# An order computed inside the kernel, and transposes moved to DMA, in a fused attention and feed-forward kernel

## The chip, the cores and the metric

The kernel runs on one core of one Trainium2 chip. The metric is the device time of one execution in microseconds (us); less is better. Each kernel was executed several times. A verdict of faster or slower needs a difference of 2%, with a 95% interval.

Names used below: PE is the matrix engine TensorE, PEld its weight loads, DVE is VectorE, ACT is ScalarE, POOL is GpSimd and SP is SyncE. SP computes nothing here; it issues DMA transfers. A letter q after an engine's name means its instruction queue.

## The reference, cut to what matters

The input `x` is 2048 x 512, in bf16. The output mixes an attention layer with memory (32 heads of width 16, four segments of 512 tokens) and a gated feed-forward layer (width 1792), with one gate value per token.

```python
g = sigmoid((x * gate_w).sum(-1))
for s in range(4):                                   # segments of 512 tokens
    p = softmax(q_s k_s^T * scale + causal mask);  a_dot = p v_s
    a_mem = phi(q_s) M / (phi(q_s) z + 1e-6)         # phi(t) = t+1 if t>0 else exp(t)
    o_s = sigmoid(beta) * a_mem + (1 - sigmoid(beta)) * a_dot
    M += phi(k_s)^T v_s;  z += sum phi(k_s)
a = o @ wo
b = (relu(x @ W_gate) * (x @ W_up)) @ W_down
out = g * a + (1 - g) * b
```

## The kernel before

A "unit" is one segment and one group of eight heads, so there are 16 units. Each unit computes scores K·Q on PE into one four-bank tile of PSUM (the accumulators' memory), takes exp of them on ACT, masks on POOL, multiplies by V on PE, combines on DVE and transposes back on PE. That is the score chain. Since it has only one four-bank tile, a fill (the score matmuls) and its exp alternate and never overlap. Other work (projections, gate and up matmuls, down matmuls) has to fill the engines in between. The framework's pools decide which buffers are shared:

```python
# PSUM: "S" one 4-bank tile for scores; "X" 2 banks; "F" 2 banks
def xT_and_gate(seg):                         # x^T by PE transposes
    for c in range(NC):
        tp = psum.tile([P, 4, P], BF16, name="tp", tag="F", bufs=2)
        for t in range(4):
            nc.tensor.transpose(tp[:, t, :], xn[:, t, c * P:(c + 1) * P], ident[:])
        nc.vector.tensor_copy(xT[:, c, seg * L:(seg + 1) * L], ...)

def proj(seg):
    ...                                       # Q; then K, dimension-major:
    for c in range(NC):
        ps = psum.tile([P, L], F32, name="ps_proj", tag="X", bufs=2)
        ...                                   # 4 matmuls wk, xT
        nc.vector.tensor_copy(KTe[:, c, :], ps[:])
        ...
    if seg < NSEG - 1:                        # K a second time, token-major, for phi(K)
        for t in range(4):
            ps = psum.tile([P, D], F32, name="ps_proj", tag="X", bufs=2)
            for ci in range(NC):
                nc.tensor.matmul(ps[:], lhsT=xT[:, ci, s0 + t * P:s0 + (t + 1) * P],
                                 rhs=wk_sb[:, ci, :], ...)
            ...                               # exp, min, max-add -> pK
    ...                                       # V

def qk_exp(seg, c):                           # 6 fills of the score tile per unit
    for kb in range(4):
        Nk = L - P * kb                       # 512, 384, 256, 128 columns
        if Nk > 256:
            for r in range(2):
                sp = psum.tile([P, 4, L], F32, name="sp", tag="S", bufs=1)
                ...                           # 4 matmuls of 32 rows, exp, mask
        else:
            ...                               # both r in one fill

for i, u in enumerate(units):                 # emission order of the main loop
    seg, c = u
    if i + 1 < len(units):
        pending_E[un] = qk_exp(*un)           # scores of the next unit
    if c == 1 and seg < NSEG - 1:             # the whole next projection, in one block
        xT_and_gate(seg + 1); proj(seg + 1); tok_gate(seg + 1)
        gate_gen[seg + 1] = ffn_gateup_items(seg + 1)
    pv_combine(seg, c, pending_E.pop(u), hook=hook)   # hook: gate/up and down matmuls
    ...
```

The softmax here doesn't subtract the row's maximum and nothing guards it: scores larger than these inputs give would overflow.

## Time and profile before

| | before |
|---|---|
| median of 3 runs | 353.75 us (353.05 to 354.65) |
| span of the profiled execution | 351.7 us |
| PE busy | 308.4 us (88%) |
| first exp of the score chain starts | 30.0 us |
| last exp ends | 329.3 us, so the chain takes 299.3 us for 96 fills |
| after the last exp | 22.4 us |

The profile page first. The first lines give busy time and share of the span by engine. The rows of digits cut the span into 40 slices; a digit is the busy share in tenths, and PEclk is PE's granted clock. The last line is the chain of waits, followed back from the end.

```profile
span 351.7 us, 7235 instructions
...
PE 308.4 (88%) x2941; PEld 148.1 (42%) x2992; DVE 229.1 (65%) x684; ACT 198.0 (56%) x187; POOL 90.5 (26%) x153
...
PE   3489988899999799898999988888999989989984
...
DVE  2557959788422756989835575899845386766253
...
PE 52%; DVE 30%; ACT 7%; DMA 5%; issue 3%; POOL 0%; SPq 0%; DVEq 0%; ACTq 0%
```

PE is busy, but often only at 8 tenths, and 30% of the chain of waits is DVE. PE's largest waits, by what ended them (total us, times, longest):

```profile
PE ndt L343 <- DVE o_sb L342: 9.8, 17, 1.4
PE tp L174 <- DMA xn<-in_A_x_dram: 5.7, 1, 5.7
PE ups L383 <- DMA wu_sb<-in_B_W_up_dram: 5.0, 1, 5.0
```

PE loses about 11 us at the start to two transfers, and 9.8 us in 17 small waits where the transpose of an output block waits for DVE. Now two stretches of the span. The columns are busy us and instructions of PE, PEld, DVE, ACT and POOL, then clock, DMA share and GB/s.

```profile
8.00:20.00 12.00, 6.02 (x26) 2.29 (x25) 5.47 (x15) 3.12 (x6) 0.00 (x0) 0.97 1.05 348
145.00:168.70 23.70, 21.60 (x184) 10.56 (x186) 21.69 (x62) 8.39 (x14) 3.97 (x6) 1.00 0.07 24
```

From 145 to 168.7 us (the projection of a new segment) DVE is busy for 21.69 of 23.7 us, ACT for only 8.39. What the score chain does is shown by ACT's timeline (start, length, instruction, and in brackets the idle time before it and what ended it):

```profile
148.10 1.02 ACT L286 ACTIVATE E_1851<-sp 128x1024 bf16<-128x1024 f32 x1 [0.50 <-PE sp L255]
...
165.00 0.60 ACT L387 ACTIVATE rg<-gps 128x512 bf16<-128x512 f32 x1 [2.07 <-PE ndt L343]
168.69 1.88 ACT L276 ACTIVATE E_2271<-sp 128x2048 bf16<-128x2048 f32 x1 [3.10 <-PE ndt L317]
...
171.07 1.88 ACT L276 ACTIVATE E_2271<-sp 128x2048 bf16<-128x2048 f32 x1
```

Between the exp at 148.10 and the one at 168.69 there is none for 19.6 us; ACT runs only small pieces of other work. Two full exps of a unit can start 2.4 us apart (168.69 to 171.07); over the whole chain a step takes 3.1 us on average (299.3 us for 96).

### The profile page before, as it was taken

Reading aid. Unit: us, or ns where it says so; the run is one execution under the profiler, and the core shown is the slowest. Engines: PE = TensorE matmul, PEld = TensorE weight load, DVE = VectorE, ACT = ScalarE, POOL = GpSimd, SP = SyncE. Lnnn points to the kernel's source line nnn. Section 1 sums busy time; section 2 is a strip of 40 time slices with the busy share of each in tenths; the row PEclk is TensorE's granted clock in tenths of the full one; section 3 lists DMA queues with packets and bytes.
Section 4 is the critical chain, followed back from the end, with each engine's and each line's share of the span. In section 5 each row is a group of like instructions: output and inputs, shape, how many; then the busy total and the mean of one; then the engine's idle time right before and its main releaser. Section 6 shows DMA issues by size and latency. Waiting matters only on the chain.

```text
span 351.7 us, 7235 instructions
## 1 busy us (share of the span) xinstructions
PE 308.4 (88%) x2941; PEld 148.1 (42%) x2992; DVE 229.1 (65%) x684; ACT 198.0 (56%) x187; POOL 90.5 (26%) x153
## 2 busy tenths in 40 slices
PE   3489988899999799898999988888999989989984
PEld 2133343335444344334644444334544444444452
DVE  2557959788422756989835575899845386766253
ACT  1306578755843687831754577841764378886300
POOL 6000343341321424310231144230231133242300
PEclk9989999999999999999999999999999999999999
DMA  7991100001000000001000000000000000000000
GB/s 195 357 335 55 61 2 0 2 1 62 3 16 16 32 2 0 2 0 61 2 2 17 30 18 3 0 2 0 2 3 17 30 17 2 0 2 3 0 32 30
DMA packets 10209, 12.39 MB, mean 35 GB/s; under 512 B 593, under 2 KB 9313, under 8 KB 10177
## 3 DMA queue, kind: packets, MB, share of 16 engines
q1 hardware_dynamic: 7584, 6.82, 6.1%
q0 software_dynamic: 1008, 3.55, 3.3%
q10 hardware_dynamic: 1584, 1.57, 1.4%
q8 instruction: 23, 0.38, 0.4%
q14 instruction: 10, 0.07, 0.1%
HBM read 9.84 MB, written 2.10 MB: 34 GB/s over the span
## 4 chain that ended last, share of the span: by engine, by line
PE 52%; DVE 30%; ACT 7%; DMA 5%; issue 3%; POOL 0%; SPq 0%; DVEq 0%; ACTq 0%
PE acc L398 14%; PE ups L383 9%; PE gps L378 7%; PE ndt L317 6%; DMA wu_sb<-in_B_W_up_dram 5%; PE sp L255 4%; DVE hT L388 4%; DVE tb L339 3%; DVE osb L411 3%; PE ps_proj L242 2%; PE ndt L343 2%; PE acc L408 2%; DVE coef L337 2%; PE ps_proj L230 2%; DVE rsb L335 2%
## 5 line engine op out<-in xcount | busy, mean ns | idle before, releaser
L383 PE MATMUL ups<-xT,wu_sb 128*128 128x512 bf16 x210 | 62.7, 382 | 7.1 <-DMA wu_sb<-in_B_W_up_dram 5.0
L378 PE MATMUL gps<-xT,wg_sb 128*128 128x512 bf16 x205 | 59.8, 380 | 2.3 <-DMA wg_sb<-in_B_W_gate_dram 1.0
L388 DVE TENSOR_TENSOR hT<-ups,rg 128x512 bf16<-128x512 f32 x56 | 38.3, 684 | 24.2 <-PE ups L383 18.5
L387 ACT ACTIVATE rg<-gps 128x512 bf16<-128x512 f32 x56 | 33.5, 598 | 35.7 <-PE gps L378 27.8
L398 PE MATMUL acc<-wd_sb,hT 128*128 128x512 bf16 x217 | 50.3, 379 | 0.9 <-DVE osb L411 0.2
L398 PEld LDWEIGHTS <-hT 128*128 128x128 bf16 x224 | 21.5, 98 | 25.3 <-issue 1.2
L383 PEld LDWEIGHTS <-wu_sb 128*128 128x128 bf16 x224 | 20.1, 98 | 25.5 <-DMA wu_sb<-in_B_W_up_dram 5.5
L345 DVE CAST oT<-ndt 128x128 bf16<-128x128 f32 x64 | 18.3, 286 | 16.4 <-PE ndt L343 16.4
L411 DVE TENSOR_SCALAR osb<-acc,ngcol 128x512 bf16<-128x512 f32 x16 | 12.0, 750 | 22.5 <-PE acc L408 22.5
L378 PEld LDWEIGHTS <-wg_sb 128*128 128x128 bf16 x224 | 18.3, 97 | 18.2 <-issue 3.7
L343 PE MATMUL ndt<-diag_134,o_sb 128*128 128x128 bf16 x64 | 14.5, 226 | 11.4 <-DVE o_sb L342 9.8
L333 DVE TENSOR_TENSOR dsb<-ndt,epsvec 128x16 f32<-128x16 f32 x48 | 8.1, 169 | 24.2 <-PE ndt L317 23.7
L255 PE MATMUL sp<-QTsb,KTe 32*128 32x512 bf16 (+3 forms) x256 | 21.7, 304 | 0.7 <-issue 0.2
L339 DVE TENSOR_TENSOR tb<-ndt,coef 128x256 bf16<-128x256 f32 x48 | 20.2, 421 | 1.3
L255 PE MATMUL sp<-QTsb,KTo 32*128 32x512 bf16 (+3 forms) x256 | 20.2, 299 | 0.6 <-ACT E_3100 L276 0.2
L408 PE MATMUL acc<-wo_sb,oT 128*128 128x512 bf16 x60 | 17.8, 380 | 2.3 <-DVE oT L345 1.9
L218 PE MATMUL ps_proj<-xT,wk_sb 128*128 128x512 bf16 x64 | 17.1, 396 | 2.3 <-DVE KTe L221 0.9
L242 PE MATMUL ps_proj<-wv_sb,xT 128*128 128x512 bf16 x62 | 15.7, 379 | 2.6 <-DVE pK L236 1.1
L343 PEld LDWEIGHTS <-o_sb 128*128 128x128 bf16 x64 | 6.1, 95 | 27.6 <-DVE o_sb L342 23.1
L204 PE MATMUL ps_proj<-xT,wq_sb 128*128 128x512 bf16 x61 | 17.1, 393 | 0.5
L255 PEld LDWEIGHTS <-KTe 32*128 32x128 bf16 x256 | 7.1, 91 | 24.1 <-issue 22.9
L207 DVE CAST QTsb<-ps_proj 128x512 bf16<-128x512 f32 x16 | 10.8, 685 | 3.8 <-PE ps_proj L204 3.8
(468 smaller groups left out, 708.6 us busy)
## 6 DMA issues: line engine op xcount, KB each, us to landing
out_dram<-osb SPq DMA_DIRECT2D x16, 128.0 KB, 1.7
xn<-in_A_x_dram POOLq DMA_DIRECT2D x3, 512.0 KB, 3.8
wd_sb<-in_B_W_down_dram POOLq DMA_DIRECT2D x2, 640.0 KB, 12.4
wg_sb<-in_B_W_gate_dram SPq DMA_DIRECT2D x2, 512.0 KB, 14.2
wu_sb<-in_B_W_up_dram SPq DMA_DIRECT2D x2, 512.0 KB, 18.2
wg_sb<-in_B_W_gate_dram SPq DMA_DIRECT2D x2, 384.0 KB, 13.2
wu_sb<-in_B_W_up_dram SPq DMA_DIRECT2D x2, 384.0 KB, 8.8
xn<-in_A_x_dram SPq DMA_DIRECT2D x1, 512.0 KB, 4.9
```

Of the source, the lines that this page charges most:

```text
L242: nc.tensor.matmul(ps[:], lhsT=xT[:, ci, s0 + t * P:s0 + (t + 1) * P], rhs=wv_sb[:, ci, :], start=(ci == 0), stop=(ci == NC - 1))
L255: nc.tensor.matmul(out_ap, lhsT=ktile[32 * j:32 * j + 32, c, kb * P:(kb + 1) * P], rhs=st["QTsb"][32 * j:32 * j + 32, c, kb * P:kb * P + N ...
L317: nc.tensor.matmul(ndm[:, 0, hl8, 0:DH + 1], lhsT=E[kb][:, es, (qb - kb) * P:(qb - kb + 1) * P], rhs=st["Vp"][:, kb, h, 0:DH + 1], start=f ...
L339: nc.vector.tensor_tensor(tb[:], ndm[:, :, :, 0:DH], coef[:, :, :, None].to_broadcast([P, 2, 8, DH]), ALU.mult)
L343: nc.tensor.matmul(trp, lhsT=o_sb.rearrange("p h e -> p (h e)"), rhs=diag16[:, t, :], start=True, stop=True)
L378: nc.tensor.matmul(gps[:], lhsT=wg_sb[:, ci, fv * P:(fv + 1) * P], rhs=xT[:, ci, s0:s0 + L], start=(ci == 0), stop=(ci == NC - 1))
L383: nc.tensor.matmul(ups[:], lhsT=wu_sb[:, ci, fv * P:(fv + 1) * P], rhs=xT[:, ci, s0:s0 + L], start=(ci == 0), stop=(ci == NC - 1))
L387: nc.scalar.activation(rg[:], gps[:], ACT.Relu)
L388: nc.vector.tensor_tensor(hT[:, fv, :], ups[:], rg[:], ALU.mult)
L398: nc.tensor.matmul(acc[:], lhsT=hT[:, fv, lc:lc + P], rhs=wd_sb[:, fv, :], start=(fv == 0), stop=False)
L408: nc.tensor.matmul(acc[:], lhsT=oT[:, ci, lc:lc + P], rhs=wo_sb[:, ci, :], start=False, stop=(ci == NC - 1))
L411: nc.vector.tensor_scalar(osb[:], acc[:], ngcol[:, tt:tt + 1], None, ALU.mult)
```

## The change

The intent is to keep PE busy without gaps. The kernel no longer leaves the order to the framework. It describes all work as tasks with an engine, a duration, a key of priority and dependences; a list scheduler in the kernel then fixes the order of every engine and the choice of PSUM banks. The score chain of a unit gets keys two units early (`LEAD`), so it always goes first; gate, up, down and projections are the filler. Along with this:

- x^T comes by a transposing DMA, and so does token-major phi(K), which makes the second K projection (48 matmuls) needless.
- Five full fills (4 x 512 columns) per unit take the place of six partly short ones: 80 in all, not 96.
- Four PSUM banks are one pool for all work outside the score tile; rings for Q, K, E and h are deeper.
- The token gate moves from DVE to 64 one-column matmuls; combines take two query blocks at once; one copy of 512 columns takes the place of four for o^T.
- The first weights are split, several weights move to the GpSimd queue, and nine warm-up matmuls run first.

The diff, cut to its core (cuts are marked `...`):

```diff
-HP = 18
+RQ = 6
+RE = 8
+RH = 18
+class Plan:
+    def run(self):
+        ...
+                for t in sorted((t for t in ready if t.avail <= now), key=lambda t: t.key):
+                    if busy.get(t.eng, 0.0) > now:
+                        continue
+                    if t.need is not None and not t.need.banks:
+                        got = self.pick(t.need, now)
+                        ...
+                    order.append(t)
+    ...
+    ctx.enter_context(tc.manual_schedule())
...
+    clock = [3000.0]
+    def arrival(nbytes):
+        clock[0] += nbytes / 380.0
+        return plan.add("in%d" % len(plan.tasks), 0.0, 0.0, None, lat=clock[0])
+    def load_xT(seg):
+        nc.sync.dma_start_transpose(out=xT[:, :, seg * L:(seg + 1) * L],
+                                    in_=x[seg * L:(seg + 1) * L, :])
+        return arrival(L * D * 2)
...
-    load_x(nc.sync, 0)
-    load_w_piece(nc.scalar, wq_sb, A_wq, 0, D)
-    load_w_piece(nc.scalar, wk_sb, A_wk, 0, D)
-    load_w_piece(nc.scalar, wv_sb, A_wv, 0, D)
...
+    got_x[0] = load_xT(0)
+    got_q = [load_cols(nc.scalar, wq_sb, A_wq, 0, 256)]
+    got_k = [load_cols(nc.scalar, wk_sb, A_wk, 0, 256)]
...
+    got_v = load_cols(nc.sync, wv_sb, A_wv, 0, D)
+    got_g[0] = load_cols(nc.sync, wg_sb, B_W_gate, *FP[0])
+    got_u[0] = load_cols(nc.sync, wu_sb, B_W_up, *FP[0])
+    got_x[1] = load_xT(1)
+    for i in range(1, 4):
+        got_g[i] = load_cols(nc.gpsimd, wg_sb, B_W_gate, *FP[i])
+        got_u[i] = load_cols(nc.gpsimd, wu_sb, B_W_up, *FP[i])
+    got_x[2] = load_xT(2)
+    got_x[3] = load_xT(3)
+    got_d = [load(nc.gpsimd, wd_sb[:, a:b, :], ...) for a, b in ((0, 7), (7, NF))]
+    got_o = load_cols(nc.gpsimd, wo_sb, A_wo, 0, D)
...
-            pK = segpool.tile([P, 4, D], BF16, name="pK", bufs=2)
-            for t in range(4):
-                ...
-                    nc.tensor.matmul(ps[:], lhsT=xT[:, ci, s0 + t * P:s0 + (t + 1) * P],
-                                     rhs=wk_sb[:, ci, :], ...)
+        prj["pk", seg, c] = plan.add("SP", 1300, key + 500, lambda: nc.sync.dma_start_transpose(
+            out=pK[i][:, :, c * P:(c + 1) * P], in_=pk[0][:]),
+            [b] + [att.get(("mz", seg - 2))], 2000)
...
+    FILLS = [[(0, 0, 0)], [(1, 0, 0)], [(0, 1, 0), (0, 3, 384)], [(1, 1, 0), (1, 3, 384)],
+             [(0, 2, 0), (1, 2, 256)]]
...
+    LEAD, FLAG, RL = 2.0, 0.0, 40000.0
+    for k in range(9):
+        nc.tensor.matmul(wb[3][:], lhsT=junk[:, 0:P], rhs=junk[:], start=True, stop=True)
+    order = plan.run()
+    for t in order:
+        if t.emit is not None:
+            t.emit()
```

The plan assumes that transfers land one after another in the order in which they are written down, at 380 bytes per ns from 3 us on.

## The prediction

> **What bounds the kernel now.** The page gives a span of 351.7 us with TensorE (PE) 88% busy, DVE 65%, ACT 56%; the chain of waits is 52% PE and 30% DVE. I count work, not busy time. In the timeline dense 128x512 matmuls start 216 ns apart, 32 P·V matmuls take 0.81 us, and a score fill of four 32-row tiles holds PE about 0.33 us, or 0.43 us where it cuts into other work. The Trainium skill ("TensorE: Matmul & The Clock Gate", "Wait — 56ns, not 53.3ns?") states 215.7 ns for 512 columns; this trace agrees. My PE sum for before is about 290 us. The missing 60 us: about 12 us in the first 20 us (windows view: PE busy 8.2 us, waiting for x, then the up weights), 6 us in the last 27 us, and about 40 us in between (11.4 us before the transposes of o, for DVE).
>
> **What the change removes and adds, estimated.**
> - PE: minus 48 second-K-projection matmuls (10.4 us) and 64 x transposes (0.71 us per 8: 5.7 us), plus 64 one-column gate matmuls (1.6 us). New sum: gate/up 97, down 48, four projections 55, scores 80 x 0.43 = 34, P·V 33, rest 11: about 278 us.
> - DVE: minus x^T copies (6.5), gate reductions (12.5), part of the combines (62.7 to about 48), of the oT copies (18.3 to 11), of the memory update (12 to 4): 229 to about 190 us.
> - ACT: five full fills of 1.88 us per unit (150 us in all) replace 9.55 us per unit; total 198 to about 195. The score chain is serial through one 4-bank tile: 80 x (1.88 + 0.43 + 0.35 signalling) = 213 us, about 260 with residual waits for a busy PE and ACT. It nears the PE bound, not more.
> - DMA transposes: 4 of 512 KB, 12 of 128 KB. The skill ("DMA: Bandwidth & Descriptors", "Latency and other measured facts") gives 261 GB/s, so an estimate of 2 us plus overhead for x; no trace shows one yet. The x load of before landed in 4.9 us; I expect 5 to 9.
>
> **What is on the critical path.** PE is nearly saturated, so the 14.5 us removed from it count fully; DVE work counts only through bubbles. The pinned order puts gate/up, down and the next projections as filler behind the score chain, with interchangeable banks and deeper rings. I expect 25 to 30 us of the 40 us of middle bubbles to go. Smaller first weight pieces and no PE transpose save 3 to 4 us at the start.
>
> **Prediction.** 278 PE + 10 start + 3 tail + 7 bubbles = **298 us, range 287 to 314**. Chances: faster by over 2% 0.96, within 2% 0.02, slower 0.02.
>
> **What would show it right.** PE busy well over 90% from about 12 us to the end; DVE about 190 us, ACT about 195; PE's largest wait in the middle no longer the o transposes; the chain mostly PE; x^T landing under 9 us; phi(K) transposes done long before the memory update.
>
> **What would make it wrong.** A pinned order cannot react: if a transfer lands later than planned, PE stands at the head of its queue though other work is ready. The x transpose could take 15 us. The score chain could be the bound, with ACT at every fill behind relu: then about 310. With nearly no bubbles: about 288.

## The result, and the profile after

| | before | after |
|---|---|---|
| median of the runs made side by side | 353.63 us (353.05 to 354.65) | 312.74 us (312.32 to 312.97) |
| ratio | | 0.8838 (0.882 to 0.8856): faster |
| span profiled | 351.7 us | 311.0 us |
| PE busy | 308.4 (88%) | 290.3 (93%) |
| DVE busy | 229.1 | 185.1 |
| ACT busy | 198.0 | 192.7 |
| first exp starts | 30.0 | 22.1 |
| first exp to last exp | 299.3 (96 fills) | 258.1 (80 fills) |
| after the last exp | 22.4 | 30.8 |

All outputs are right. Here and below, "gain" is the difference of medians, 353.63 - 312.74 = 40.9 us. The last three rows sum up to the span, so they split the 40.7 us by which the span fell: 7.9 from an earlier start of the score chain, 41.2 from a shorter chain, and 8.4 given back after it.

The page of after, the same lines (with the clock and the GB/s rows, which matter now):

```profile
PE 290.3 (93%) x2953; PEld 140.9 (45%) x2953; DVE 185.1 (60%) x458; ACT 192.7 (62%) x166; POOL 96.2 (31%) x150
...
PE   5646799999999999999999999999999999999995
...
DVE  0236287957688153977884549594879271838211
...
PEclk9989599999999999999999999999999999999999
...
GB/s 135 257 333 342 193 25 37 34 2 4 19 0 36 2 34 37 2 17 2 13 6 19 36 18 19 3 0 2 2 0 2 20 19 34 2 0 2 2 34 34
...
PE 80%; DMA 8%; DVE 7%; SPq 2%; ACT 1%; issue 1%; DVEq 0%; ACTq 0%
```

From the sixth slice on PE stands at 9, to the last slice but one. The weak part is the first five slices, 39 us, and these are also the slices with the most DMA traffic. The chain of waits is now 80% PE, and its second item is DMA. PE's waits:

```profile
PE wb_124 L321 <- DMA xT<-in_A_x_dram: 5.0, 1, 5.0
PE wb_125 L391 <- DMA wv_sb<-in_A_wv_dram: 4.6, 1, 4.6
PE wb_125 L321 <- DMA xT<-in_A_x_dram: 4.2, 1, 4.2
...
PE sp L404 <- ACT E_160 L425: 0.3, 1, 0.3
```

The three waits that matter are all for transfers at the start: x^T of segment 1 (5.0 us), the V weights (4.6) and x^T of segment 0 (4.2). Nothing after them is over 0.3 us (a wait of 1.9 us for a memset at the very start aside). The 9.8 us of waits for the o transposes are gone. By stretches:

```profile
0.00:10.00 10.00, 4.02 (x9) 1.34 (x10) 0.72 (x7) 1.28 (x1) 6.10 (x12) 1.00 0.95 128
10.00:20.00 10.00, 5.44 (x16) 1.87 (x15) 3.52 (x7) 1.31 (x3) 6.29 (x10) 1.00 1.09 327
20.00:33.30 13.30, 8.21 (x48) 3.02 (x49) 6.26 (x17) 4.35 (x3) 1.85 (x2) 0.78 1.07 323
33.30:36.00 2.70, 2.69 (x13) 0.67 (x13) 0.16 (x1) 0.79 (x2) 0.00 (x0) 0.50 1.70 182
...
50.00:300.00 250.00, 248.48 (x2688) 124.06 (x2686) 161.46 (x395) 173.76 (x147) 77.64 (x119) 1.00 0.06 13
```

PE is busy for 248.48 of 250 us from 50 to 300, but from 0 to 33.3 only for 17.7 us, and some of that is warm-up. In 33.3 to 36.0, after the wait of 5.0 us, the granted clock is 0.50. The Trainium skill ("TensorE: Matmul & The Clock Gate", "What's actually happening") says that the array falls to half its clock after an idle window of about 3.4 us; this trace agrees. ACT's timeline in the middle, where before had its gap:

```profile
143.98 1.88 ACT L425 ACTIVATE E_158<-sp 128x2048 bf16<-128x2048 f32 x1 [1.66 <-PE sp L404]
...
147.31 1.87 ACT L425 ACTIVATE E_159<-sp 128x2048 bf16<-128x2048 f32 x1
...
150.66 1.87 ACT L425 ACTIVATE E_160<-sp 128x2048 bf16<-128x2048 f32 x1
...
153.68 1.87 ACT L425 ACTIVATE E_161<-sp 128x2048 bf16<-128x2048 f32 x1
```

An exp starts about every 3.2 us while a new segment's projections run alongside. That is also the mean step of the whole chain (258.1 us for 80), no shorter than before's 3.1: the chain is shorter because it has fewer steps and no long gaps, while its exps are all full ones. In the whole chain after has one gap of over 3 us between exps (7.8 us at 28.0 us, while PE waits for x^T), before had 11.

Why were the transfers late? The timeline of the start: some of the issues (start, length of the issue, queue that issues), and the first matmuls that need x^T:

```profile
0.81 1.40 SPq L186 DMA_TRANSPOSE xT<-in_A_x_dram  x1
...
2.28 2.06 SPq L177 DMA_DIRECT2D wv_sb<-in_A_wv_dram  x1
...
2.78 0.75 POOL L177 DMA_DIRECT2D wg_sb<-in_B_W_gate_dram  x1
...
7.68 29.40 SPq L186 DMA_TRANSPOSE xT<-in_A_x_dram  x3
10.04 1.86 PE L321 MATMUL wb_125<-xT,wq_sb 128*128 128x512 bf16 x4 [4.16 <-DMA xT<-in_A_x_dram]
```

And the share of the queues (packets, MB), with q1 the queue of SP and q0 that of GpSimd:

```profile
q1 hardware_dynamic: 18736, 7.34, 11.6%
q0 software_dynamic: 1424, 4.99, 5.0%
```

Landing times, read from the trace per tile: x^T of segment 0 at 10.0 us (9.2 us after its issue), the V weights at 20.1 (issued at 2.28), the first gate and up pieces at 27.2 and 31.2, x^T of segment 1 at 33.3 (25.6 us after its issue at 7.68). In the same time six gate and up pieces on the GpSimd queue, none of them needed yet, landed at 14 to 22 us. So late-needed data went ahead of urgent data.

### The profile page after: what moved, and what is told of

It is laid out like the page before. It is cut to its first block, busy times and chain, and to the rows that moved or that the text cites. A ratio compares the mean times of both kernels' runs of the same rounds, so it can differ in the third digit from the quotient of the medians.

```text
span 311.0 us, 6988 instructions
## 1 busy us (share of the span) xinstructions
PE 290.3 (93%) x2953; PEld 140.9 (45%) x2953; DVE 185.1 (60%) x458; ACT 192.7 (62%) x166; POOL 96.2 (31%) x150
## 3 DMA queue, kind: packets, MB, share of 16 engines
q1 hardware_dynamic: 18736, 7.34, 11.6%
q0 software_dynamic: 1424, 4.99, 5.0%
## 4 chain that ended last, share of the span: by engine, by line
PE 80%; DMA 8%; DVE 7%; SPq 2%; ACT 1%; issue 1%; DVEq 0%; ACTq 0%
PE wb_123 L550 9%; DMA xT<-in_A_x_dram 8%; PE wb_122 L573 8%; PE sp L404 8%; PE wb_125 L550 7%; PE wb_124 L550 6%; PE wb_122 L550 6%; PE wb_123 L573 6%; PE wb_124 L453 4%; PE wb_122 L453 3%; PE wb_122 L586 2%; PE wb_123 L321 2%; PE wb_122 L321 2%; PE wb_124 L321 2%; PE wb_123 L586 2%; SPq L177 2%
## 5 line engine op out<-in xcount | busy, mean ns | idle before, releaser
L550 PEld LDWEIGHTS <-wg_sb 128*128 128x128 bf16 x224 | 20.0, 97 | 23.4 <-issue 3.2
L550 PEld LDWEIGHTS <-wu_sb 128*128 128x128 bf16 x224 | 18.8, 98 | 23.1 <-issue 7.0
L425 ACT ACTIVATE E_154<-sp 128x2048 bf16<-128x2048 f32 x10 | 18.7, 1874 | 9.6 <-PE sp L404 8.3
L425 ACT ACTIVATE E_155<-sp 128x2048 bf16<-128x2048 f32 x10 | 18.8, 1876 | 7.7 <-PE sp L404 7.7
L425 ACT ACTIVATE E_158<-sp 128x2048 bf16<-128x2048 f32 x10 | 18.8, 1876 | 7.7 <-PE sp L404 5.0
L425 ACT ACTIVATE E_157<-sp 128x2048 bf16<-128x2048 f32 x10 | 18.8, 1881 | 7.2 <-PE sp L404 6.3
L425 ACT ACTIVATE E_159<-sp 128x2048 bf16<-128x2048 f32 x10 | 18.8, 1876 | 6.5 <-PE sp L404 5.2
L425 ACT ACTIVATE E_160<-sp 128x2048 bf16<-128x2048 f32 x10 | 18.8, 1876 | 4.5 <-PE sp L404 4.5
L425 ACT ACTIVATE E_161<-sp 128x2048 bf16<-128x2048 f32 x10 | 18.8, 1875 | 4.1 <-PE sp L404 3.7
L425 ACT ACTIVATE E_156<-sp 128x2048 bf16<-128x2048 f32 x10 | 18.8, 1876 | 4.1 <-PE sp L404 4.1
L550 PE MATMUL wb_123<-xT,wu_sb 128*128 128x512 bf16 x76 | 19.6, 381 | 0.0
L431 POOL TENSOR_SCALAR_AFFINE_SELECT E_154<-E_154 128x512 bf16<-128x512 bf16 x16 | 10.9, 696 | 26.3 <-ACT E_154 L425 26.3
L431 POOL TENSOR_SCALAR_AFFINE_SELECT E_156<-E_156 128x512 bf16<-128x512 bf16 x16 | 10.4, 663 | 27.8 <-ACT E_156 L425 27.8
L550 PE MATMUL wb_125<-xT,wg_sb 128*128 128x512 bf16 x72 | 18.5, 379 | 0.0
L431 POOL TENSOR_SCALAR_AFFINE_SELECT E_158<-E_158 128x512 bf16<-128x512 bf16 x16 | 10.7, 682 | 22.8 <-ACT E_158 L425 22.8
L431 POOL TENSOR_SCALAR_AFFINE_SELECT E_157<-E_157 128x512 bf16<-128x512 bf16 x16 | 10.5, 669 | 21.3 <-ACT E_157 L425 21.3
L431 POOL TENSOR_SCALAR_AFFINE_SELECT E_155<-E_155 128x512 bf16<-128x512 bf16 x16 | 10.5, 670 | 20.1 <-ACT E_155 L425 20.1
L431 POOL TENSOR_SCALAR_AFFINE_SELECT E_160<-E_160 128x512 bf16<-128x512 bf16 x16 | 10.4, 665 | 20.1 <-ACT E_160 L425 20.1
L550 PE MATMUL wb_123<-xT,wg_sb 128*128 128x512 bf16 x64 | 16.5, 380 | 0.1
L431 POOL TENSOR_SCALAR_AFFINE_SELECT E_161<-E_161 128x512 bf16<-128x512 bf16 x16 | 10.5, 670 | 19.7 <-ACT E_161 L425 19.7
L431 POOL TENSOR_SCALAR_AFFINE_SELECT E_159<-E_159 128x512 bf16<-128x512 bf16 x16 | 10.1, 646 | 20.6 <-ACT E_159 L425 20.6
L594 DVE TENSOR_SCALAR osb<-wb_122,ngcol 128x512 bf16<-128x512 f32 x8 | 6.0, 750 | 15.9 <-PE wb_122 L586 15.9
## 6 DMA issues: line engine op xcount, KB each, us to landing
wg_sb<-in_B_W_gate_dram POOLq DMA_DIRECT2D x2, 384.0 KB, 13.8
wv_sb<-in_A_wv_dram SPq DMA_DIRECT2D x1, 512.0 KB, 17.8
```

The costliest lines, as they stand in the source:

```text
L425: b = plan.add("ACT", 1880, key, lambda Ef=Ef: nc.scalar.activation(Ef[:], sp[:], ACT.Exp, scale=SCALE), [a] + eread.get(n - RE, []), ACL)
L431: nc.gpsimd.affine_select(out=m, in_=m, compare_op=ALU.is_ge, fill=0.0, base=0, pattern=[[0, 4], [1, P]], channel_multiplier=-1)
L550: nc.tensor.matmul(bank(sl), lhsT=w[:, ci, fv * P:(fv + 1) * P], rhs=xT[:, ci, seg * L:(seg + 1) * L], start=(ci == 0), stop=(ci == NC - 1))
L594: nc.vector.tensor_scalar(osb[0][:], bank(sl), ngcol[:, tt:tt + 1], None, ALU.mult)
```

## The experiments

The questions were three: where the 14.7 us between the prediction of 298 and the result went; whether the PE work that was removed counts; and which part of the change made the middle dense. On the first there were three theories. The first: urgent transfers share bandwidth with late-needed ones that go ahead on another queue. A rival: the transposing DMA is slow by itself. Another: the plan assumed wrong arrival times, so that a fixed order stood waiting with other work ready. The texts call these three A, B and C.

In the runs, `first exp + chain + tail` gives the profiled span split as in the table above. Twelve kernels were run, in three batches, each beside runs of the kernel before on the same chip (medians 353.66, 353.72 and 354.06). The kernel after was not run again in these batches, so "above after" and "below after" compare batches; before's medians differ by at most 0.4 us between them. Differences from after of under 2% (replan, split_banks, h14) are clear of the spread of the runs. Some traces lack about 50 matmul records; for those I use waits and the chain, not PE's busy sum.

### bulk_on_sp: late-needed weights behind the urgent ones

```diff
     for i in range(1, 4):
-        got_g[i] = load_cols(nc.gpsimd, wg_sb, B_W_gate, *FP[i])
-        got_u[i] = load_cols(nc.gpsimd, wu_sb, B_W_up, *FP[i])
+        got_g[i] = load_cols(nc.sync, wg_sb, B_W_gate, *FP[i])
+        got_u[i] = load_cols(nc.sync, wu_sb, B_W_up, *FP[i])
...                                   # the same for got_d and got_o
```

The plan and with it the order of every compute engine is that of after.

> The changed kernel with one edit: the bulk weights (gate and up from the second piece on, down, out) are issued from the SP queue behind the first ones instead of from the GpSimd queue beside them. The pinned order of every engine is the same. Theory A (the 15 us that the prediction missed lie in the first 36 us, because bulk weights that are needed late share the bandwidth with x^T, wv and the first gate and up pieces): x^T of segment 1 lands before 25 us instead of 33.3, wv before 16 us instead of 20.1, and the time falls from 312.7 to 300-307. Rival B (the transposing DMA is slow by itself, order does not matter): x^T of segment 1 still lands after 30 us and the time stays within 2 us.

Measured: 298.23 us, ratio 0.8433 (0.8413 to 0.8453), 14.5 us below after and a little better than expected; 15.8 + 250.0 + 30.6. The V weights landed at 13.2 us, x^T of segment 1 at 17.8 (10.5 us after issue; its issuing instruction took 8.5 us, not 23.2). PE's waits over 0.5 us:

```profile
PE wb L321 <- DMA xT<-in_A_x_dram: 3.8, 1, 3.8
PE wb L614 <- DVE junk L252: 1.9, 1, 1.9
PE wb L444 <- DVE tb L485: 0.6, 2, 0.5
```

Two of the three waits for transfers are gone. Nothing else was changed, so the waits at the start were the cost of the queue choice: it took 6.3 us off the time to the first exp (22.1 to 15.8) and 8.1 off the chain (258.1 to 250.0), which contained the wait for x^T of segment 1. That choice sets two things at once, when the late weights are sent and by which queue; no run sends them late on the GpSimd queue, so the two are not told apart.

### x0_alone: the first x^T with nothing beside it on other queues

On top of bulk_on_sp, the four halves of the Q and K weights go to the SP queue as well, behind x^T of segment 0.

```diff
-    got_q = [load_cols(nc.scalar, wq_sb, A_wq, 0, 256)]
-    got_k = [load_cols(nc.scalar, wk_sb, A_wk, 0, 256)]
+    got_q = [load_cols(nc.sync, wq_sb, A_wq, 0, 256)]
+    got_k = [load_cols(nc.sync, wk_sb, A_wk, 0, 256)]
...                                   # the same for columns 256 to 512
```

> As the run with the bulk on the SP queue, but all early weights too are issued on SP behind the x^T of segment 0, so that its transposing DMA runs without another large transfer beside it. Theory A (late because of shared bandwidth): x^T of segment 0 lands at 5.5-7 us instead of 9.5. Rival B (the transposing DMA is slow by itself): it still lands after 8 us. The time is 296-301 in both cases, as the first weights of Q and K come later.

Measured: 296.52 us (296.3 to 297.9), ratio 0.8391 (0.8365 to 0.8416); 15.6 + 250.0 + 30.7. x^T of segment 0 now landed 5.9 us after its issue, at 6.7 us, against 9.2 us in after and 8.7 in bulk_on_sp. PE now waits for the Q weights instead:

```profile
PE wb L321 <- DMA wq_sb<-in_A_wq_dram: 1.9, 1, 1.9
```

So 3.3 of the 9.2 us come from what runs on other queues beside it. The 5.9 us that remain are at the low end of the 5 to 9 us predicted; they are not a floor, as smaller weights still followed on SP's queue and a later x^T of the same size landed 4.1 us after its issue (bulk_warm_replan). Together with x^T of segment 1 (25.6 us after issue in after, 10.5 in bulk_on_sp) this says that the late landings come from the other transfers. The rival (slow by itself) falls as the reason for them, but not altogether: from 33.4 to 37.0 us in after, when only the transposing transfers of segments 2 and 3 were left in flight, the DMA engines were full (share 1.25) and moved 130 GB/s, against 342 GB/s from 20 to 28 us at a share of 1.04. So transposing transfers fill the engines at well under half that rate; how much they slow the transfers beside them was not tested. The time barely moves, since PE then starts at 7.8 us at the cold rate and the Q weights are next in line. Against bulk_on_sp this is 1.7 us, in another batch, so it is a hint of a gain and no more. It is the fastest version that was run, 5% under after.

### replan: the plan told the real landing times

The queues stay as in after; only the plan's arrival times change, to those measured in after's trace.

```diff
+    LANDED = [10.0, 4.4, 9.8, 11.3, 15.2, 20.1, 11.4, 27.2, 31.2, 33.3, ...]
     def arrival(nbytes):
-        clock[0] += nbytes / 380.0
-        return plan.add("in%d" % len(plan.tasks), 0.0, 0.0, None, lat=clock[0])
+        n = len(plan.tasks)
+        return plan.add("in%d" % n, 0.0, 0.0, None, lat=1000.0 * LANDED[n])
```

> The changed kernel with the same DMA issues, but the list scheduler is given the landing times that the trace of the changed kernel shows (x^T 10.0 and 33.3 us, wv 20.1, first gate and up 27.2 and 31.2, the later gate pieces 14 to 22) instead of its own guesses of 4 to 12 us. Theory C (a pinned order cannot react; other work was ready while PE stood): PE's waits for wv (4.6 us) and x^T (5.0 us) go, the time falls to 302-307. If there was nothing else to do, it stays within 2 us of 312.7.

Measured: 308.36 us, ratio 0.8726 (0.8697 to 0.8754), only 4.4 us below after, a little worse than expected; 17.4 + 256.7 + 30.7.

```profile
PE wb L323 <- DMA xT<-in_A_x_dram: 4.0, 1, 4.0
PE sp L406 <- ACT E L427: 2.7, 5, 1.1
...
PE wb L455 <- ACT rg L561: 1.5, 1, 1.5
```

The waits for transfers shrank to one of 4.0 us, but new waits for ACT came up in the middle, 2.7 us before score fills (after had 0.3 and 0.2) and 1.5 us before other work. So the order did cost waits at the start (13.8 us in after, 4.0 here), but the new plan lost about as much again in the middle as it kept: 4.4 us is what is left of both, and not the cost of the wrong order alone. In this plan a better order did not make up for late data; mending the transfers gave more (bulk_on_sp, 14.5 us).

### bulk_warm_replan: three remedies at once

bulk_on_sp, plus the landing times of that run in the plan, plus 22 warm-up matmuls in place of 9.

```diff
+    LANDED = [9.5, 3.9, 8.9, 10.9, 12.3, 13.2, 11.0, 14.6, 16.1, 17.8, ...]
...                                   # arrival() as in replan, queues as in bulk_on_sp
-    for k in range(9):
+    for k in range(22):
```

> The version meant to be best: bulk weights on the SP queue, the list scheduler given the landing times that this order of issue showed (x^T 9.5 and 17.8 us, wv 13.2, first gate and up 14.6 and 16.1), and 22 warm-up matmuls instead of 9, so that PE's clock is full when x^T lands at 9.5 us (in the run with the bulk on SP, PE ran at half clock from 9.6 to about 13 us: 1.5 us lost). Expected 294-298 against 298.2; if the new order brings back waits for ACT and DVE, as the other run with corrected landing times did, 298-300.

Measured: 302.2 us, ratio 0.8548 (0.8514 to 0.8582): 4 us slower than bulk_on_sp alone. The expectation missed. 16.3 + 253.7 + 30.6: the chain is 3.7 us longer.

```profile
PE sp L406 <- ACT E L427: 2.9, 6, 1.1
PE wb L323 <- DMA xT<-in_A_x_dram: 2.2, 1, 2.2
```

The warm-ups worked: here the first projections of four matmuls start 0.86 us apart, against 1.7 us in after (0.43 us per matmul, the cold spacing that the Trainium skill states as 426.7 ns for 512 columns in "TensorE: Matmul & The Clock Gate", "Wait — 56ns, not 53.3ns?"). But PE waits 2.9 us for ACT before score fills, where bulk_on_sp has 0.5. An order from truer times was worse in the middle. A greedy list order moves by some us when its inputs change; why this one came out worse is open.

### before_one_k: one K projection in the kernel before

```diff
         for c in range(NC):
             ...                      # K, dimension-major
+            if pK is not None:
+                e1 = workpool.tile([P, L], BF16, name="e1")
+                nc.scalar.activation(e1[:], ps[:], ACT.Exp)
+                nc.vector.tensor_scalar(e1[:], e1[:], 1.0, None, ALU.min)
+                nc.vector.scalar_tensor_tensor(e1[:], ps[:], 0.0, e1[:], ALU.max, ALU.add)
+                nc.sync.dma_start_transpose(out=pK[:, :, c * P:(c + 1) * P], in_=e1[:])
-            for t in range(4):       # the second, token-major projection
-                ...
```

> The kernel before with one part of the change: no second K projection; phi(K) is computed from the transposed K that is there already and turned by 12 transposing DMAs of 128 KB. 48 matmuls (10.4 us of PE work) go, everything else and the framework's own ordering stay. If removed PE work counts in before as it did in the changed kernel (8.6 us for the same 48 matmuls), 353.6 falls to 343-346. If before is held up by its waits rather than by PE work, the gain is under 4 us.

Measured: 352.67 us, ratio 0.9963 (0.9931 to 0.9994): 1.0 us, where 10.4 us of PE work was removed. In the stretch of the projection (same columns as above):

```profile
145.00:168.00 23.00, 18.89 (x170) 9.20 (x168) 21.03 (x68) 7.87 (x12) 3.89 (x6) 0.93 0.19 47
```

PE is busy for 18.89 us of 23, DVE for 21.03. Before had 21.60 and 21.69 of 23.7. The PE work went, the stretch stayed: DVE paces it in both, by this reading. That DVE is the pace, and not the order in which the two X banks are handed round, is read from windows and not isolated; the edit leaves the work of DVE as it was (229.2 us in all, before 229.1), and adds 12 transposing transfers to the path.

### before_less_pe: also x^T by DMA in the kernel before

On top of before_one_k, x^T comes by `dma_start_transpose` on SP, and the PE transposes and their copies are deleted. (x is still loaded for the gate.)

```diff
-    load_x(nc.sync, 0)
+    load_xT(0)                       # dma_start_transpose
+    load_x(nc.gpsimd, 0)
...
-            for t in range(4):
-                nc.tensor.transpose(tp[:, t, :], xn[:, t, c * P:(c + 1) * P], ident[:])
-            nc.vector.tensor_copy(xT[:, c, seg * L:(seg + 1) * L], ...)
```

> As before_one_k, and x^T by transposing DMA as well, so both parts of the change that take work off PE (10.4 + 5.7 us) and 6.5 us off DVE, in the kernel before. The x^T of segment 0 should land at 9 to 10 us (before: x at 5.7 us and then PE transposes until 8 us), so 1 to 2 us are lost at the start. Expected 338-343 if PE work counts; if the late x^T or the missing slack eats it, no better than before_one_k.

Measured: 357.73 us, ratio 1.0115 (1.0078 to 1.0152), 4.0 us above the before of its batch (under 2%), where 338 to 343 was expected if PE work counts; 36.4 + 296.1 + 23.0.

```profile
PE ps_proj L206 <- DMA xT<-in_A_x_dram: 14.0, 1, 14.0
PE ndt L341 <- DVE o_sb L340: 10.4, 19, 1.4
```

The start lost 6.3 us, since PE waits 14.0 us for the transposing DMA that shares the start with the other first loads; the chain is 3.2 us shorter. About 16 us of PE work was removed in all, and the kernel is not faster. In the kernel before, taking this work off PE did not shorten the time.

### k_twice: the removed matmuls put back into after

```diff
-        a = plan.add("PE", 864, key, lambda: proj_mm(sl, wk_sb, c, seg), ...
+        def kk():
+            if seg < NSEG - 1:
+                proj_mm(sl, wk_sb, c, seg)
+            proj_mm(sl, wk_sb, c, seg)
+        a = plan.add("PE", 864, key, kk, ...
```

The result stays right, since the second group overwrites the first.

> The changed kernel, but each K projection of the first three segments is computed twice into the same bank (the second run overwrites the first), 48 matmuls of 216 ns more in the same pinned order: the work that the second K projection of before cost. If PE is saturated in the middle, the time rises by 10.4 us (9 to 11.5) to 323; if there is slack, by less than 6.

Measured: 321.34 us, ratio 0.9085 (0.9067 to 0.9102): 8.6 us above after for the same 48 matmuls (10.4 us of work) that were worth 1.0 us in before. The missing 1.8 us fit the start, where the extra work filled waits: those for x^T and the V weights are 11.6 us here and 13.8 in after. With PE dense, PE work counts almost fully in this kernel.

### unpinned: the same emission order, but the framework orders

```diff
-    ctx.enter_context(tc.manual_schedule())
```

> The changed kernel without the statement that pins the order: the same operations, banks and rings, but the framework's own scheduler orders each engine. If the pinned order is what removed the bubbles in the middle, PE's idle time after 40 us rises from about 1.5 us to 10 us or more and the time to 325-340. If the larger rings, wider combines and the removed PE work did it, the time stays within 5 us of 312.7, or falls, as this order starts from other guesses of the transfers.

Measured: 321.15 us, ratio 0.9078 (0.9063 to 0.9092): 8.4 us above after, between the two expectations; 21.4 + 267.4 + 30.8. All of it is in the chain (plus 9.3). The pinning is worth 8.4 us on top of the plan's emission order. The larger part of the gain does not need it.

### lead0: the score chain without its lead

```diff
-    LEAD, FLAG, RL = 2.0, 0.0, 40000.0
+    LEAD, FLAG, RL = 0.0, 0.0, 40000.0
```

> The changed kernel, but the score chain no longer has its lead: the keys of the list scheduler put scores and exp of a unit two units later than now, so that PE takes gate, up and down matmuls earlier and scores later. If what counts is that the serial score chain (258 us from its first to its last exp in the changed kernel) starts early and always goes first, the filler runs out before the chain ends and the time rises by 8 us or more, with PE idle in the last 30 us; if PE's total work is all that counts, the time stays within 3 us of 312.7.

Measured: 342.18 us, ratio 0.9675 (0.9652 to 0.9699): 29.4 us above after, 72% of the gain given back by one number. 35.5 + 276.3 + 28.3. Of the loss, 13.3 us are a later first exp, at the start where the transfers are late (PE waits 13.7 us for x^T and the V weights here, 13.8 in after, but does its scores later); 18.2 us are a longer chain, and the tail is 2.5 us shorter. ACT's timeline shows what happens in the chain:

```profile
178.13 1.88 ACT L425 ACTIVATE E<-sp 128x2048 bf16<-128x2048 f32 x1
194.98 1.88 ACT L425 ACTIVATE E<-sp 128x2048 bf16<-128x2048 f32 x1 [14.97 <-PE sp L404]
```

Fifteen us without an exp, while PE is busy for 14.95 of the 15 us from 180 to 195, with 76 matmuls, mostly down work that had the better key. Near the end the filler is used up, and from 300 to 318 us only the rest of the chain runs, before the last down matmuls that need its output: from 300 to 320 us PE is busy for 9.89 of 20 us at a granted clock of 0.50. The work is the same; only its order differs.

### six_fills: six fills per unit, as before had them

```diff
-    FILLS = [[(0, 0, 0)], [(1, 0, 0)], [(0, 1, 0), (0, 3, 384)], [(1, 1, 0), (1, 3, 384)],
-             [(0, 2, 0), (1, 2, 256)]]
+    FILLS = [[(0, 0, 0)], [(1, 0, 0)], [(0, 1, 0)], [(1, 1, 0)],
+             [(0, 2, 0), (1, 2, 256)], [(0, 3, 0), (1, 3, 128)]]
...
-                         [got_x[seg], got_g[piece]], PEL, need=gsl)
+                         [got_x[seg], got_g[piece]] + hread.get(NF * seg + fv - RH, []), PEL, need=gsl)
```

The second hunk was needed: without it the scheduler took all banks for work that could not finish, and got stuck. So this run holds that dependence as well.

> The changed kernel, but with six score fills per unit as in before (512, 512, 384, 384, 2 x 256, 2 x 128 columns) instead of five full ones: 16 more steps of the serial chain fill, exp, fill; ACT's exp work 9.55 instead of 9.4 us per unit, PE's columns the same. (One dependency is added so that the list scheduler doesn't get stuck: a gate matmul waits until its h buffer is free.) If PE bounds the middle, the time rises by 1 to 4 us. If the serial score chain bounds it, each of 16 more steps costs about 0.8 us or more: 12 us or more, to 325.

Measured: 324.89 us, ratio 0.9197 (0.9145 to 0.9249): 12.2 us above after. 22.5 + 273.8 + 26.6. Exp is busy for 153 us, against 150 in after, so the cost is the 16 extra steps (a step takes 2.85 us on average now), not the exp itself. With 96 fills, as many as before, the chain takes 273.8 us and not 299.3: of the 41.2 us by which after shortened it, 15.7 us come with the five fills (and without the added dependence), 25.5 with all the rest. The windows:

```profile
50.00:280.00 230.00, 227.56 (x2430) 112.67 (x2429) 148.85 (x365) 164.11 (x151) 71.79 (x109) 1.00 0.05 14
290.00:300.00 10.00, 5.96 (x113) 3.88 (x111) 4.54 (x15) 4.82 (x4) 3.34 (x6) 0.78 0.01 2
300.00:310.00 10.00, 8.59 (x32) 3.56 (x32) 1.23 (x3) 0.00 (x0) 0.00 (x0) 0.71 0.01 2
```

PE is dense to 280 us, then 5.96 of 10 us at clock 0.78. The chain's last exp ends at 296.4 us, and the filler ran out before it. So chain and filler are near balance in after: a chain 15.7 us longer is already the bound.

### split_banks: the four shared banks as two and two

```diff
-        ok = [b for b in sorted(self.free) if self.free[b] is not None and self.free[b] <= now]
+        ok = [b for b in sorted(self.free) if self.free[b] is not None and self.free[b] <= now
+              and b // 2 == slot.side]
...                                   # side 1: gate, up and down; side 0: all else
```

> The changed kernel, but the four shared PSUM banks are split as in before: two for gate, up and down, two for projections, P.V, transposes of o and the memory. The list scheduler makes its order under that limit. If the shared pool is a main part of the gain, PE idles in the middle (over 8 us after 36 us) and the time rises to 325-345; if not, it stays within 5 us of 312.7.

Measured: 309.64 us, ratio 0.8746 (0.8726 to 0.8766): 3.1 us below after. 16.9 + 264.4 + 26.4. The middle is the same: PE is busy for 228.79 of 230 us from 50 to 280, against 228.78 in after. The gain comes from the start, where this plan lets PE do more: it is busy for 22.95 of the first 36 us, in after for 20.35, and the first exp comes 5.2 us earlier (the chain is then 6.3 us longer and the tail 4.4 shorter). The shared pool shows no worth in time here.

### h14: a ring of 14 chunks of h, as before

```diff
-RH = 18
+RH = 14
...                                   # and the dependence of six_fills' second hunk
```

> The changed kernel with 14 buffers for h instead of 18, as many as before had, so that gate and up of the next segment wait for the down matmuls of this one (a gate matmul waits until its h buffer is free, so that the plan doesn't get stuck). If the deeper ring of h is a main part of the gain, PE idles at the ends of segments and the time rises by over 8 us; if not, by under 4 us.

Measured: 318.56 us, ratio 0.9013 (0.8984 to 0.9041): 5.8 us above after. 22.8 + 259.5 + 32.4. It lies between the thresholds of the two theories, and it includes the added dependence, so it is inconclusive on how much the deeper ring is worth.

## Why the prediction was right or wrong

The direction was right, and 312.7 us lies in the range of 287 to 314, near its upper end and 14.7 us above 298. Term by term, for the profiled span of 311.0 us:

| term | predicted | measured | how read |
|---|---|---|---|
| PE work | 278 | 281.1 | span minus the three below (slack inside PE's busy time falls in here) |
| lost at the start | 10 | 24.8 | 36.0 us, in which only about 11.2 us of dense work was done (11 groups of four matmuls at 0.864, ten projections and one of gate weights; 3 fills of 0.4; the token gate 0.5); cold clock and warm-up count as lost |
| bubbles in the middle | 7 | 1.5 | PE idle, 36 to 307.5 us |
| tail | 3 | 3.55 | last PE work to the end of the span |

The differences sum up to 13; the other 1.7 us is device time outside the profiled span. That the sum stayed in the range has some luck in it: the bubbles came out 5.5 us better than predicted and paid for part of the 14.8 us lost at the start; without that the time would have been about 318.

- **The step that failed** is "Smaller first weight pieces and no PE transpose save 3 to 4 us at the start", the term "10 start". It measured 24.8 us. Against before nothing was saved at all: in the first 36 us PE was busy for 23.4 us in before, and in after for 16.3 us, the warm-up of 4.0 left out. The prediction costed the x^T transfer alone (5 to 9 us) and never asked what the other queues would have in flight. x^T of segment 0 landed at 10.0 us, and the V weights and the second x^T, which were not costed, at 20.1 and 33.3. Moving the late-needed weights behind the urgent ones gave 14.5 us back (bulk_on_sp, 298.2 us), and by the same count PE was then busy for 26.2 us, 2.8 more than in before and close to the saving of 3 to 4 that had been predicted. The warning "if a transfer lands later than planned, PE stands at the head of its queue though other work is ready" named the risk. replan, where the order knew the real times, took 9.8 us off these waits but kept only 4.4 us of time, as new waits came up in the middle.
- **"PE is nearly saturated, so the 14.5 us removed from it count fully"** was wrong of the kernel before. There the removed K projection is worth 1.0 us (before_one_k), and with the transposes gone too the kernel is 4.0 us slower, through its start. In after the same 48 matmuls cost 8.6 us (k_twice). The sum came out right because the change also made PE dense, and only then did less PE work pay. lead0 shows that the order is needed for that; whether the 44 us taken off DVE is needed too, no run shows.
- **"25 to 30 us of the 40 us of middle bubbles to go"** was too careful: 1.5 us are left from 36 us on. What the runs show to matter is the lead of the score chain (lead0, 29.4 us, of which 18.2 in the chain), then five fills for six (12.2 us, including an added dependence) and the pinning (8.4 us). These overlap and don't sum up to the gain. The "interchangeable banks", which the prediction named as a cause, give nothing (split_banks).
- **The score chain "about 260", "not more" than the PE bound**: it measured 258.1 us, and 250.0 in bulk_on_sp, without the wait for x^T of segment 1. six_fills shows how close the two are.
- **Checks**: PE is 93% busy, and dense from 36 us, not from 12. DVE is 185.1 us (190 predicted), ACT 192.7 (195). The wait for the o transposes is gone. The chain is 80% PE. "x^T landing under 9 us" failed (10.0). The transposes of phi(K) landed 2.5 us after issue, and no wait of PE for them shows.

Open: how much of before's gaps is DVE's work in the projection block and how much its place in the order; what the 44 us less of DVE work (wider combines, single o^T copies, the token gate on PE) are worth, which were never put back alone; why truer arrival times gave a worse order; and what h14's 5.8 us consist of.

## What to carry to other kernels

When two dependent resources limit a kernel (here a serial score chain and a dense PE), give the serial chain priority with a lead and use everything else as filler; in this kernel only a dense PE turned removed PE work into time. Before trusting a start-up plan, list every transfer in flight on every queue with the moment at which it is needed, and queue late-needed data behind urgent data; a free queue for bulk loads lets them overtake. An order fixed from assumed arrival times should be checked against the landing times of a trace, but the transfers are to be mended before the order.

## What the Trainium skill lacked or had wrong

- **"DMA: Bandwidth & Descriptors", "Issuing engines are not separate DMA queues"** says that queues of different engines share the same 16 DMA engines and interleave, and that issuing from several engines only saves time on the sequencer, usually little. The first half agrees with the trace. The second lacks the loss: putting late-needed weights on the GpSimd queue, in place of behind the urgent ones on SP, cost 14.5 us of 312.7. The same page's "Queues, rings and completion order" says that a DMA engine takes turns between queues packet by packet. By the queue lines above, a packet of the GpSimd queue held 3.5 KB on average over the run and one of the SP queue 0.4 KB (4.99 MB in 1424, 7.34 MB in 18736), which would let the bulk move faster; that is argued from the page and the counts, and no run isolates it.
- **The same page, "Latency and other measured facts"**, gives 261 GB/s for a transposing DMA with a non-contiguous middle dimension, measured on one kernel. No run shows such a rate at these sizes: the fastest 512 KB from DRAM landed 4.1 us after issue (bulk_warm_replan), 128 GB/s with all fixed cost, and after moved 130 GB/s while only such transfers were in flight; the first x^T took 5.9 us with nothing large on another queue and 9.2 beside others. 128 KB between buffers on the chip took 2.5 us.
- **"DMA: Bandwidth & Descriptors"** has issue times of a transposing DMA, but none, and no other page has one, for when the queues are loaded: the instruction held SP for 1.4 us for the first x^T, but 23.2 us for the second in after and 8.5 us in bulk_on_sp, and whatever SP has to issue next waits behind it.
- **"TensorE: Matmul & The Clock Gate"** was right where it was tested: half clock after a wait of 5.0 us, 0.43 us per cold matmul. What no page has: the granted-clock column of the profile used here does not show the cold start. It reads 1.00 from 0 to 10 us, where nine matmuls took 4.02 us.
